# One change to a fused attention and expert-routing kernel: two routings search a grid with a proof, VectorE turns the rows, ScalarE reorders what is gathered

## The chip, the cores and the metric

The kernel runs on one core of a Trainium2 chip. That core has five engines that run their own instruction streams and wait for each other on semaphores: TensorE (PE in the profile, and PEld for its weight loads), VectorE (DVE), ScalarE (ACT), GpSimd (POOL) and SyncE (SP, which only issues DMAs here). The metric is the device time of one execution in microseconds (us), lower is better.

## The reference

Everything is float32. Attention with a sigmoid in the place of the softmax comes first; its output is regrouped to one row of 768 numbers for each of 3584 tokens; then a router gives each token to one of eight experts, each of which takes exactly 448 tokens.

```
q, k, v: 8 batches x 12 heads x 448 tokens x 64
attn = sigmoid(q k^T / 8 - log(448));  a = attn v
x = a regrouped to (8*448, 12*64) = (3584, 768)
logits = x @ w_gate                          # 3584 x 8
for idx in argsort(-logits.flatten()):       # best logits first
    tok, e = idx // 8, idx % 8
    if tok has an expert or expert e has 448 tokens: continue
    give tok to e
out[tokens of e] = relu(x[tokens of e] @ w1[e]) @ w2[e]   # 768 -> 1024 -> 768
```

The kernel does the greedy assignment one expert at a time: a token belongs to its best expert among those left, and the expert whose 448th best token has the highest logit is full first. It gets its tokens, is taken out, and the rest is routed again.

## The kernel before, in words

**Attention.** Batches and pairs of heads are walked in 48 iterations. VectorE turns the loaded q and k (`turn`, L408, tile `nkq` to `kqT`), ScalarE and VectorE split them in a high and a low part (L416, L417), TensorE makes the scores (`scores` L433, `rest_scores` L443), ScalarE the sigmoid (L423), TensorE the product with v (`av`, L457 and L463), VectorE copies it to SBUF (L465, L467) as `xt`: 128 head columns by 448 tokens. `logits` (L478) multiplies that with the gate. After each iteration one entry of a list `bg` is written, so small work is spread over the iterations.

**Rows.** The experts need rows by token, so `xt` is transposed and stored to the DRAM buffer `xs`. `rows` (L484) does half a chunk of 112 tokens: three TensorE transposes (L489), one copy (L492 by ScalarE or L494 by VectorE), and after the second half a DMA (L496). Batch 0 goes through `bg` during attention; the last `LATE = 7` batches, 56 half chunks, go to a list `late`, which is written between the steps of the first routing.

**Routing.** `Router.phase(k)` finds the k-th expert and its tokens. `keys` makes a key of each token for its best expert; `search` (L162) finds each expert's 448th largest key bit by bit: 16 steps, each with three thresholds counted by VectorE (L178), a sum over the partitions of an expert (for the first routing a TensorE matmul, L190; for the others VectorE transposes, L194 to L200), and a few one-column operations that set the next three thresholds. `pick` chooses the expert with the largest such key and the tokens at or above it, `place` and `lists` make the index list (`r_idx`, L298). SyncE reads the expert's number (`r_ei`) and loads its weights; GpSimd gathers the token rows from `xs` (L625).

**Experts.** For expert kx, `xturn` (L628) transposes the gathered rows by TensorE (L639) and splits them by ScalarE and VectorE; `moe` runs the two matrix products (L734 to L738 and L771 to L775), 144 matmuls each (the first of an expert in four groups of 36, the second in three of 48), and writes the result back through transposes and indirect DMAs. The generator `moe` yields after each matmul; a clock that adds 189 ns for each decides when a step of the next routing is written (`T_STEP`, `T_DVE` and the like are its due times), when gathers and transposes of the next expert are due (`prepare`, L820: gathers at once, transposes after a lag of 5 to 14 us, all left ones flushed at the end of the expert), so the program order is fixed when the kernel is built.

Of the kernel before, what the change touches and what calls it, by code (L numbers as in the profile page):

```python
# [36 lines left out]
Y_DVE, Y_WAIT = 6, 4000  # L37

# [10 lines left out]
def route_consts(nc, cp, K):  # L49
# [66 lines left out]
    K.gfin = _s32(g)  # L116


class Router:
# [4 lines left out]
    def __init__(self, tc, K, st, wk, psum):  # L124
# [5 lines left out]
        tc.nc.vector.memset(self.csum, -28.0)  # L130

# [30 lines left out]
    def search(self, pe):  # L162

        nc, K, wk, KT = self.nc, self.K, self.wk, self.KT
        p = self.bank()
        for g in range(2):
            nc.tensor.transpose(p[:, g * 112:(g + 1) * 112],
                                KT[:, g].rearrange("p e c -> p (e c)"), K.ident[:112, :112])
        KE = wk.tile([128, 224], F32, name="r_KE")
        nc.vector.tensor_copy(KE, p[:, :224])  # L170
        T, JP = K.c0, None
        X = None if pe else self.bank().bitcast(I32)
        for st in range(16):
            sh = 30 - 2 * st
            cnt = wk.tile([128, 3], BF, name="r_cnt") if pe else K.CN
            for i in range(3):
                junk = wk.tile([128, 224], BF, name="r_junk")
                nc.vector.tensor_scalar(junk, KE, T[:, i:i + 1].bitcast(F32), None, OP.is_ge, OP.add,  # L178
                                        accum_out=cnt[:, i:i + 1])
            nX = None  # L180
            if 0 < st < 15:
                nX = wk.tile([128, 3], I32, name="r_X") if pe else X[:, 4 * (st % 2):4 * (st % 2) + 3]
            acc = wk.tile([128, 1], F32, name="r_acc")
            j2 = wk.tile([128, 3], F32, name="r_j2")
            if pe:
                if nX is not None:
                    nc.vector.tensor_scalar(nX, K.kk[:, st + 1], JP, None, OP.bitwise_xor)
# [4 lines left out]
            else:  # L192
                ct = wk.tile([128, 32], F32, name="r_ct")
                nc.vector.transpose(ct, cnt)  # L194
                if nX is not None:
                    nc.vector.tensor_scalar(nX, K.kk[:, st + 1], JP, None, OP.bitwise_xor)
                s2 = wk.tile([128, 2], F32, name="r_s2")
                nc.vector.tensor_reduce(s2, ct.rearrange("p (e r) -> p e r", r=16), AX.X, OP.add)
                ct2 = wk.tile([128, 32], F32, name="r_ct")
                nc.vector.transpose(ct2.rearrange("p (e r) -> p e r", r=16), s2[:, :, None].to_broadcast([128, 2, 16]))  # L200
# [18 lines left out]
            if not pe:  # L219
                yield T_DVE  # L220
# [666 lines left out]
```

## Time and profile before

| what | value |
|---|---|
| median of 3 runs | 883.39 us (881.88 to 885.36) |
| profiled execution, whole time | 883.43 us |
| its span, first to last instruction | 881.7 us, granted clock 0.987 |
| PE busy | 840.1 us (95%) |
| DVE / ACT / POOL busy | 542.4 / 447.3 / 466.0 us |
| DMA traffic | 122.16 MB, mean 139 GB/s |
| attention (to the last `av`) | 0 to 278 us |
| first routing, gather and transposes | 278 to 333 us |
| eight experts | 333 to 862 us, then write-back |

"Busy" counts instructions in flight; a time in angle brackets after `<-` names what ended an idle time. All profile times are from the start of the span.

### The profile page before, as it was taken

How to read it: one execution, taken by the hardware profiler on the slowest of the kernel's cores; microseconds unless marked ns; L12 is line 12 of the kernel's file. 1: busy time of each engine (PE TensorE's matmuls, PEld its weight loads, DVE VectorE, ACT ScalarE, POOL GpSimd, SP SyncE). 2: the span in 40 equal slices, each digit the busy share in tenths (PEclk: the TensorE clock that was granted, in tenths of full speed). 3: DMA queues.
4: the chain of work that ended last, by engine and by line, in shares of the span. 5: the costliest groups of instructions: out<-in, count | busy, mean ns of one | idle time of the engine just before them, and what ended most of it. 6: DMA issues, size and time to landing. Idle time of an engine off the chain costs nothing.

```text
span 881.7 us, 16211 instructions
## 1 busy us (share of the span) xinstructions
PE 840.1 (95%) x5467; PEld 636.9 (72%) x5467; DVE 542.4 (62%) x2060; ACT 447.3 (51%) x612; POOL 466.0 (53%) x446
## 2 busy tenths in 40 slices
PE   6999999999999739998999999999999999999996
PEld 3455555555554528987988988988888888999996
DVE  4566555555554988958859879779779631332130
ACT  6777677777775734434434434534434344541420
POOL 9744344444410014854864873873883883851561
PEclk9999999999999979998999999999999999999999
DMA  9866766666621855443442442551542542634643
GB/s 173 165 142 149 153 126 127 127 126 127 126 43 54 270 192 154 120 138 123 128 136 97 160 155 81 177 162 57 189 153 72 170 153 90 209 96 141 203 151 126
DMA packets 213811, 122.16 MB, mean 139 GB/s; under 512 B 153344, under 2 KB 202496, under 8 KB 213728
## 3 DMA queue, kind: packets, MB, share of 16 engines
q1 hardware_dynamic: 200992, 87.62, 38.2%
q0 software_dynamic: 10880, 33.28, 12.0%
q8 instruction: 43, 0.70, 0.3%
q10 hardware_dynamic: 1856, 0.23, 0.2%
q14 instruction: 40, 0.33, 0.1%
HBM read 96.76 MB, written 24.31 MB: 137 GB/s over the span
## 4 chain that ended last, share of the span: by engine, by line
PE 82%; DVE 11%; issue 2%; DMA 2%; POOL 1%; SPq 1%; ACT 1%; POOLq 0%; DVEq 0%; ACTq 0%
PE tp L457 13%; PE sc L433 11%; PE sc L736 9%; PE sc L734 9%; PE sc L738 9%; PE sc L773 6%; PE sc L775 6%; PE sc L771 6%; DVE r_junk L178 4%; PE tp L463 2%; PE sc L443 2%; PE tp L639 2%; PE tp L652 2%; PE tp L478 1%; PE rt L289 1%
## 5 line engine op out<-in xcount | busy, mean ns | idle before, releaser
L605 POOL TENSOR_TENSOR wl<-wr,wh 128x768 fp32r<-128x768 f32 (+1 forms) x96 | 204.9, 2145 | 124.5 <-ACT wh L603 116.8
L423 ACT ACTIVATE at<-sc,bias 128x896 f32<-128x896 f32 x168 | 161.5, 1006 | 67.1 <-PE sc L443 38.4
L383 POOL DMA_DIRECT2D nkq<-in_q_dram x188 | 118.4, 646 | 116.2 <-DVE kqT L408 104.6
L775 PE MATMUL sc<-hh,wl 128*128 128x448 f32 (+2 forms) x400 | 150.2, 375 | 0.0
L738 PE MATMUL sc<-xh,wl 128*128 128x448 f32 (+2 forms) x396 | 146.2, 369 | 0.0
L736 PE MATMUL sc<-xl,wh 128*128 128x448 f32 (+2 forms) x396 | 146.0, 369 | 0.1
L773 PE MATMUL sc<-hl,wh 128*128 128x448 f32 (+2 forms) x400 | 145.5, 364 | 0.2 <-POOL hl L746 0.2
L734 PE MATMUL sc<-xh,wh 128*128 128x448 f32 (+2 forms) x396 | 145.0, 366 | 0.0
L771 PE MATMUL sc<-hh,wh 128*128 128x448 f32 (+2 forms) x400 | 144.1, 360 | 0.4 <-issue 0.4
L178 DVE TENSOR_SCALAR_CACHE_REDUCE r_junk<-r_KE,r_T 128x224 bf16<-128x224 f32 x315 | 123.2, 441 | 0.1
L603 ACT ACTIVATE wh<-wr 128x768 fp32r<-128x768 f32 (+1 forms) x112 | 102.0, 939 | 36.3 <-DMA wr<-in_moe_w_dram 23.4
L457 PE MATMUL tp<-at,nv 128*64 128x448 f32 x576 | 118.8, 548 | 0.0
L746 POOL TENSOR_TENSOR hl<-yt,hh 128x896 fp32r<-128x896 f32 x32 | 68.4, 2136 | 48.8 <-ACT yt L745 47.2
L742 ACT ACTIVATE hh<-sc 128x896 fp32r<-128x896 f32 x32 | 29.5, 921 | 117.1 <-PE sc L738 117.1
L417 DVE TENSOR_TENSOR kqL<-kqT,kqH 128x896 fp32r<-128x896 f32 (+1 forms) x49 | 52.5, 1073 | 58.5 <-ACT kqH L416 58.4
L773 PEld LDWEIGHTS sc<-hl,wh 128*128 128x128 f32 x400 | 75.8, 189 | 6.8 <-issue 1.1
L625 POOL DMA_INDIRECT xr<-xs,r_idx x32 | 32.0, 999 | 91.2 <-ACT wh L603 80.2
L736 PEld LDWEIGHTS sc<-xl,wh 128*128 128x128 f32 x396 | 75.2, 190 | 6.7 <-issue 0.5
L457 PEld LDWEIGHTS tp<-at,nv 128*64 128x64 f32 x576 | 37.1, 136 | 59.1 <-issue 56.6
L734 PEld LDWEIGHTS sc<-xh,wh 128*128 128x128 f32 x396 | 75.2, 190 | 6.0
L771 PEld LDWEIGHTS sc<-hh,wh 128*128 128x128 f32 x400 | 76.0, 190 | 4.8 <-issue 0.6
L738 PEld LDWEIGHTS sc<-xh,wl 128*128 128x128 f32 x396 | 75.1, 190 | 5.3
(166 smaller groups left out, 1266.1 us busy)
## 6 DMA issues: line engine op xcount, KB each, us to landing
wr<-in_moe_w_dram SPq DMA_DIRECT2D x64, 384.0 KB, 3.0
wr<-in_moe_w_dram SPq DMA_DIRECT2D x48, 512.0 KB, 3.6
nkq<-in_k_dram SPq DMA_DIRECT2D x192, 56.0 KB, 2.6
xs<-xr SPq DMA_DIRECT2D x32, 336.0 KB, 3.3
nkq<-in_q_dram POOLq DMA_DIRECT2D x188, 56.0 KB, 2.7
nv<-in_v_dram SPq DMA_DIRECT2D x92, 96.0 KB, 2.7
ys<-yt SPq DMA_DIRECT2D x20, 112.0 KB, 1.9
nr<-in_v_dram SPq DMA_DIRECT2D x46, 32.0 KB, 2.2
```

The costliest lines, as they stand in the source:

```text
L178: nc.vector.tensor_scalar(junk, KE, T[:, i:i + 1].bitcast(F32), None, OP.is_ge, OP.add, accum_out=cnt[:, i:i + 1])
L383: qn.dma_start(t[o:o + 32, n], rws[x])
L423: nc.scalar.activation(a, p[:, :, :S], AF.Sigmoid, bias=bias, scale=1 / math.sqrt(D))
L457: nc.tensor.matmul(p[j * 64:j * 64 + 64, :S], nat["v", b, g][:, h0 + j, c, :], AT[b, pr, c][:, j, :], start=(c == 0), stop=(c == 2 and pr ...
L603: nc.scalar.activation(hi, raw[u], AF.Copy)
L605: eng.tensor_tensor(lo, raw[u], hi.bitcast(F32), OP.subtract)
L734: nc.tensor.matmul(ph[:, f, lo:hi], wh[:, a, fs], xh[:, dd, lo:hi], start=st, stop=False)
L736: nc.tensor.matmul(ph[:, f, lo:hi], wh[:, a, fs], xl[:, dd, lo:hi], start=False, stop=False)
L738: nc.tensor.matmul(ph[:, f, lo:hi], wl[:, a, fs], xh[:, dd, lo:hi], start=False, stop=en)
L771: nc.tensor.matmul(py[:, d2, :w], wh[:, a, dsl], h1, start=st, stop=False)
L773: nc.tensor.matmul(py[:, d2, :w], wh[:, a, dsl], h2, start=False, stop=False)
L775: nc.tensor.matmul(py[:, d2, :w], wl[:, a, dsl], h1, start=False, stop=(j == 1 and a == 3))
```

## The change

Four things change together.

1. The first two routings use `grid_search`: thresholds on a fixed grid (4 steps for the first, from minus to plus twice a power of two `D` set by the largest logit of the first four batches; 9 steps for the second, in the distance `D` below the first routing's key). After it, `prove` counts the tokens at or above each expert's grid point: if exactly one expert has the highest point and exactly 448 tokens reach it, the point separates the same tokens as the exact key. VectorE reads that sum into a register and jumps over `exact`, the old search, which is run only otherwise. Routings 2 to 6 keep `search`.
2. Batches 0 to 6 are turned into rows by VectorE (`turn_rows`, three transposes of 32x32 blocks for each batch, written through `bg` during attention), batch 7 alone by TensorE in the gap (`late_rows`, with larger chunks). A row in `xs` now has its 768 numbers in the order (column of a block of 128, block) and not (block, column).
3. Since the order within a row is changed, expert 0 reads the gathered rows with a step of 6 in the transposes' weight load; for experts 1 to 7 ScalarE copies each gathered block into the plain order first (`order`, 28 copies, tile `xq`).
4. A 384-byte tile `pad` moves the load buffers: `nv`, `nr` and `nkq` start at byte 256 past a multiple of 512 in each partition before, and at a multiple of 512 now. Due times and buffer counts are set anew.

```diff
-LATE = 7
-XT_BUFS = 7
+LATE = 1
+XT_BUFS = 3
+XZ_BUFS = 2
-LATE_PER_STEP = 3
-LATE_KEYS = 7
+LATE_PER_STEP = 1
+LATE_KEYS = 3
+T_GRID, T_PROVE, T_FOUND = 2290, 3000, 9000
+N_FIRST, N_FAST = 4, 9
+PAD = 96
+NONE = 1.0e30
+FOUND = 0x43E00000
+FAST = 2
+ORDER = 2500
...
+    def grid_search(self, k):
+        nc, K, wk = self.nc, self.K, self.wk
+        pe = k == 0
+        rows = range(N_FIRST) if pe else range(1, N_FAST + 1)
+        if pe:
+            T, base = K.T0, K.base0
+        else:
+            base = wk.tile([128, 1], F32, name="r_base")
+            nc.vector.tensor_scalar(base, self.km, K.D, None, OP.subtract)
...
+        for r in rows:
...
+                self.count(T[:, i:i + 1], cnt[:, i:i + 1])
...
+            if pe:
+                ahead()
                 yield T_STEP
                 pc = self.bank()
                 nc.tensor.matmul(pc[:, :3], K.G, cnt, start=True, stop=True)
...
+            nc.vector.tensor_scalar(j2, tot, 447.5, None, OP.is_ge, OP.add, accum_out=acc)
+            if more:
+                T = wk.tile([128, 3], F32, name="r_T")
+                nc.vector.scalar_tensor_tensor(T, acc.to_broadcast([128, 3]), K.kw[:, r, :1], nX, OP.mult, OP.add)
+            nb = wk.tile([128, 1], F32, name="r_base")
+            nc.vector.tensor_scalar(nb, acc, K.kw[:, r, :1], base, OP.mult, OP.add)
...
+        self.count(base, self.cnt)
...
+    def prove(self, k):
+        p = self.bank()
+        nc.tensor.transpose(p[:, :128], self.base.to_broadcast([128, 128]), K.ident)
+        nc.tensor.matmul(p[:, 128:256], self.cnt.to_broadcast([128, 128]), K.G, start=True, stop=True)
...
+        nc.vector.tensor_scalar(few, cr, 447.5, NONE, OP.is_lt, OP.mult)
+        nc.vector.tensor_tensor(kr, tr, few, OP.subtract)
+        km = self.km = wk.tile([128, 1], F32, name="r_km")
+        nc.vector.tensor_reduce(km, kr, AX.X, OP.max)
+        nc.vector.tensor_tensor(few, cr, few, OP.add)
+        nc.vector.scalar_tensor_tensor(few, kr, km, few, OP.is_equal, OP.mult)
+        ok = wk.tile([128, 1], F32, name="r_ok")
+        nc.vector.tensor_reduce(ok, few, AX.X, OP.add)
+        found = nc.vector.value_load(ok[:1].bitcast(I32))
+        with self.tc.If(found != FOUND, preferred_fallthrough_block=True, label=f"found{k}"):
+            self.exact(kr)
+            nc.vector.tensor_reduce(km, kr, AX.X, OP.max)
+        self.choose(kr[:112], km[:112])
...
+        cp.tile([128, PAD], F32, name="pad")
...
+        def turn_rows(b, pr):
+            if pr == 1:
+                XR[b] = xa.tile([128, S // 32, 32, NP], F32, name="xz", bufs=XZ_BUFS)
+            nc.vector.transpose(XR[b].rearrange("p i j r -> p r i j")[:, pr - 1:pr + 1],
+                                XT[b][:, pr - 1:pr + 1].rearrange("p r (i t) -> p r i t", t=32))
+            if pr == NP - 1:
+                for a in range(4):
+                    nc.sync.dma_start(xs[b * S:(b + 1) * S, 192 * a:192 * a + 192].rearrange("(i t) c -> t i c", t=32),
+                                      XR[b][32 * a:32 * a + 32].rearrange("t i j r -> t i (j r)"))
...
+        def order(kx, j, n):
+            xq[kx, j] = xp.tile([128, DM], F32, name="xq", bufs=2)
+            nc.scalar.copy(xq[kx, j][:n].rearrange("p (r c) -> p r c", r=ND),
+                           xg[kx, j][:n].rearrange("p (c r) -> p r c", r=ND))
...
-                nc.tensor.transpose(p[:, i * n:(i + 1) * n], xg[kx, j][:n, dd * 128:(dd + 1) * 128], ident[:n, :n])
+                xc = xq[kx, j][:n, dd * 128:(dd + 1) * 128] if kx else xg[kx, j][:n, dd::ND]
+                nc.tensor.transpose(p[:, i * n:(i + 1) * n], xc, ident[:n, :n])
...
-                lag = max(5000, min(14000, start + 40000 - t0))
+                lag = max(ORDER + 5000, min(14000, start + 40000 - t0))
```

How the instruction order moves is seen at three places. The first is VectorE at the end of the first routing's search. `r_junk` is the count over `r_KE`, `rt` a PSUM bank, `r_J` the bits found so far, `r_km` the highest key. Before, steps 15 and 16 of 16 and the start of `pick`:

```order
L178 TENSOR_SCALAR r_junk,r_cnt<-r_KE,r_T 128x224 x3
L187 TENSOR_SCALAR r_X<-c_kk,r_J 128x3
L202 TENSOR_SCALAR r_j_3933,r_acc<-rt 128x3
L215 SCALAR_TENSOR_TENSOR r_T<-r_acc,r_X 128x3
L217 TENSOR_SCALAR r_J<-r_acc,r_J 128x1
L178 TENSOR_SCALAR r_junk,r_cnt<-r_KE,r_T 128x224 x3
L202 TENSOR_SCALAR r_j_3968,r_acc<-rt 128x3
L217 TENSOR_SCALAR r_J<-r_acc,r_J 128x1
L222 TENSOR_SCALAR r_kap<-r_J 128x1
L232 TENSOR_REDUCE r_km<-rt 112x1
L234 SCALAR_TENSOR_TENSOR r_w_3998<-rt,r_km,c_rank 112x8
```

Now, the fourth and last grid step, the proof and the jump (the 181 instructions of `exact` lie behind it, and the first of `choose` after those):

```order
L186 TENSOR_SCALAR r_junk,r_cnt<-r_KE,r_T 128x224 x3
L236 TENSOR_SCALAR r_j_3511,r_acc<-rt 128x3
L241 TENSOR_SCALAR r_base<-r_acc,c_kw,r_base 128x1
L186 TENSOR_SCALAR r_junk,r_cn_3518<-r_KE,r_base 128x224
L345 TENSOR_SCALAR r_few<-rt 128x8
L346 TENSOR_TENSOR r_kr<-rt,r_few 128x8
L348 TENSOR_REDUCE r_km<-r_kr 128x1
L349 TENSOR_TENSOR r_few<-rt,r_few 128x8
L350 SCALAR_TENSOR_TENSOR r_few<-r_kr,r_km,r_few 128x8
L352 TENSOR_REDUCE r_ok<-r_few 128x1
L353 TENSOR_LOAD r_ok
L354 COMPARE_AND_BRANCH
```

Twelve of sixteen steps are gone, and one count, six small operations, a register load and a jump have come.

The second is TensorE at the end of expert 0, where the gathered rows of expert 1 are transposed. Before (`xr` are gathered rows; L771 to L775 are expert 0, L734 to L738 expert 1):

```order
L639 MATMUL tp<-ident,xr 128x128 x3
L775 MATMUL sc<-hh,wl 128x448
L771 MATMUL sc<-hh,wh 128x448
L773 MATMUL sc<-hl,wh 128x448
L775 MATMUL sc<-hh,wl 128x448
L639 MATMUL tp<-ident,xr 128x128 x9
L639 MATMUL tp<-ident,xr 128x64 x6
L734 MATMUL sc<-xh,wh 128x448
```

Now (`xq` are the rows that ScalarE has reordered; L942 to L946 are expert 0, L905 to L909 expert 1), the last two of the eight groups of transposes:

```order
L810 MATMUL tp<-ident,xq 128x64 x3
L942 MATMUL sc<-hh,wh 128x448
L944 MATMUL sc<-hl,wh 128x448
L946 MATMUL sc<-hh,wl 128x448
L942 MATMUL sc<-hh,wh 128x448
L944 MATMUL sc<-hl,wh 128x448
L946 MATMUL sc<-hh,wl 128x448
L810 MATMUL tp<-ident,xq 128x64 x3
L942 MATMUL sc<-hh,wh 128x448
L944 MATMUL sc<-hl,wh 128x448
L946 MATMUL sc<-hh,wl 128x448
L905 MATMUL sc<-xh,wh 128x448
```

Before, five of the eight groups stood in one block between the experts; now all eight stand between matmuls of expert 0, because the second routing's list is written 42 matmuls earlier.

The third is VectorE in the middle of attention. Before, two iterations (L408 and L417 prepare the next pair, L465 and L467 take the result of the last):

```order
L408 STREAM_TRANSPOSE kqT<-nkq 128x896
L417 TENSOR_TENSOR kqL<-kqT,kqH 128x896
L465 COPY xt<-tp 128x448
L408 STREAM_TRANSPOSE kqT<-nkq 128x896
L417 TENSOR_TENSOR kqL<-kqT,kqH 128x896
L465 COPY xt<-tp 128x448
L467 TENSOR_TENSOR xt<-tp,xt 128x448
```

Now:

```order
L545 STREAM_TRANSPOSE kqT<-nkq 128x896
L554 TENSOR_TENSOR kqL<-kqT,kqH 128x896
L602 COPY xt<-tp 128x448
L655 STREAM_TRANSPOSE xz<-xt 128x2x448
L545 STREAM_TRANSPOSE kqT<-nkq 128x896
L554 TENSOR_TENSOR kqL<-kqT,kqH 128x896
L602 COPY xt<-tp 128x448
L604 TENSOR_TENSOR xt<-tp,xt 128x448
```

A row transpose stands ahead of every second `kqT`, 21 times in all. The stores of a batch's rows (four DMAs, L659) stand on SyncE's queue between the loads of later pairs.

More of the change, by code (lines that the diff above doesn't have):

```diff
@@ L167, in search @@
             nc.tensor.transpose(p[:, g * 112:(g + 1) * 112],
[L168 to L174, printed above, removed]
+                                KT[:, g].rearrange("p e c -> p (e c)"), self.K.ident[:112, :112])
+        self.KE = self.wk.tile([128, 224], F32, name="r_KE")
@@ new lines, in ends, with count, sums @@
+        nc.vector.tensor_copy(self.KE, p[:, :224])
+    def count(self, T, cnt):
+        junk = self.wk.tile([128, 224], BF, name="r_junk")
+        self.nc.vector.tensor_scalar(junk, self.KE, T, None, OP.is_ge, OP.add, accum_out=cnt)
+    def sums(self, cnt, ct, s2, ct2, between=None):
+        nc = self.nc
+        nc.vector.transpose(ct, cnt)
+        if between:
+            between()
+        nc.vector.tensor_reduce(s2, ct.rearrange("p (e r) -> p e r", r=16), AX.X, OP.add)
+        nc.vector.transpose(ct2.rearrange("p (e r) -> p e r", r=16), s2[:, :, None].to_broadcast([128, 2, 16]))
+        return ct2[:, :3]
@@ new lines, in grid_search, with search, ahead @@
+            nb = wk.tile([128, 1], F32, name="r_base")
+            nc.vector.tensor_scalar(nb, acc, K.kw[:, r, :1], base, OP.mult, OP.add)
+            base = nb
+            if more and not pe:
+                yield T_GRID
+        if pe:
+            self.tc.mark_branch_hint_location(f"found{k}", "LikelyTaken", [mybir.EngineType.DVE])
+        self.base = base
+        self.cnt = wk.tile([128, 1], BF, name="r_cn1")
+        self.count(base, self.cnt)
+    def search(self):
+        nc, K, wk = self.nc, self.K, self.wk
+        T, JP = K.c0, None
+        X = self.bank().bitcast(I32)
+        for st in range(16):
+            sh = 30 - 2 * st
+            for i in range(3):
+                self.count(T[:, i:i + 1].bitcast(F32), K.CN[:, i:i + 1])
+            nX = None
+            if 0 < st < 15:
+                nX = X[:, 4 * (st % 2):4 * (st % 2) + 3]
+            acc = wk.tile([128, 1], F32, name="r_acc")
+            j2 = wk.tile([128, 3], F32, name="r_j2")
+            def ahead(st=st, nX=nX, JP=JP):
@@ L329, in phase @@
             yield T_KEYS
-            yield from self.search(k == 0)
-            yield T_KAP
-            self.pick()
+            self.ends()
+            if k < FAST:
+                yield from self.grid_search(k)
+                yield T_PROVE
+                self.prove(k)
+                yield T_FOUND
+            else:
+                yield from self.search()
+                yield T_KAP
+                self.pick()
+                yield T_PICK
         else:
             self.left()
-        yield T_PICK
+            yield T_PICK
         yield from self.place()
@@ new lines, in moe_attention, with late_rows @@
+        XR = {}
+        def late_rows(b, c):
+            x = xa.tile([CP, DM], F32, name="xr", bufs=XA_BUFS)
+            p = ps_s.tile([128, 2, 512], F32, name="sc")
+            for r in range(NP):
+                o = r % 4 * 128
+                nc.tensor.transpose(p[:CP, r // 4, o:o + 128], XT[b][:, r, c * CP:(c + 1) * CP], ident)
+            xv = x.rearrange("p (c r) -> p r c", r=NP)
+            for h, n in ((0, 4), (1, 2)):
+                nc.scalar.copy(xv[:, 4 * h:4 * h + n], p[:CP, h, :128 * n].rearrange("p (r c) -> p r c", r=n))
+            nc.sync.dma_start(xs[b * S + c * CP:b * S + (c + 1) * CP], x)
@@ L531, in moe_attention @@
                     bg.append(lambda b=b: logits(b, range(NP)))
-                for c in range(NCH):
-                    for hf in range(2):
-                        if b >= B - LATE:
-                            late.append(lambda b=b, c=c, hf=hf: rows(b, c, hf, "act"))
-                        else:
-                            bg.append(lambda b=b, c=c, hf=hf: rows(b, c, hf, "dve"))
+                if b == 3:
+                    bg.append(scale)
+                for c in range(NCH if b >= B - LATE else 0):
+                    late.append(lambda b=b, c=c: late_rows(b, c))
         for f in bg:
```

141 lines of the change are left out of this document (97 added, 44 removed).

## The prediction

> **What bounds the kernel now.** I read the table of stages first (from, to, length, then busy time and instruction count of PE, PEld, DVE, ACT and POOL, granted clock, DMA share, GB/s).
>
> ```profile
> 0.00:278.00 278.00, 270.40 (x2216) 137.88 (x2216) 152.35 (x210) 199.82 (x220) 128.30 (x220) 1.00 0.62 126
> 278.00:333.00 55.00, 34.47 (x257) 23.05 (x257) 45.48 (x223) 29.85 (x63) 4.13 (x6) 0.88 0.68 218
> 333.00:400.00 67.00, 66.86 (x399) 59.86 (x398) 53.60 (x284) 26.23 (x39) 41.09 (x22) 1.00 0.45 137
> 400.00:412.00 12.00, 9.36 (x39) 7.40 (x39) 9.42 (x50) 4.59 (x10) 2.97 (x4) 0.72 0.13 45
> 412.00:862.00 450.00, 446.93 (x2462) 397.30 (x2461) 279.77 (x1296) 184.63 (x277) 285.43 (x187) 1.00 0.44 140
> ```
>
> Attention and the experts are TensorE's: it idles 7.6 us of 278 and 3.1 of 450. The two stages in which it is not the bound are the gap of 55 us, where DVE is busy for 45, and the 12 us around 400, with the clock at 0.72. The chain of waits (start, length, what) says what fills the gap:
>
> ```profile
> 285.12 0.52 DVE r_junk L178 x3
> ...
> 287.66 1.20 DVE r_junk L178 x6
> ...
> 311.75 1.11 DVE r_junk L178 x6
> ...
> 313.60 1.11 DVE r_junk L178 x6
> ...
> 326.70 4.49 DMA xr<-xs,r_idx
> ```
>
> The sixteen search steps follow one another at 1.85 us (313.60 - 311.75) with nothing between, then the token list, then the gather. The row transposes of seven batches that PE does meanwhile (L489) are only cover: nothing in the chain after 285 is theirs.
>
> **First routing.** The timeline (start, length, engine, line; in brackets the idle time and its releaser) ends the search so:
>
> ```profile
> 315.97 0.17 DVE L232 TENSOR_REDUCE r_km<-rt 112x1 f32<-112x8 f32 x1 [0.41 <-PE rt L229]
> 316.17 0.23 DVE L234 SCALAR_TENSOR_TENSOR r_w<-rt,r_km,c_rank 112x8 f32<-112x8 f32 x1
> 316.43 0.16 DVE L236 TENSOR_REDUCE r_c<-r_w 112x1 f32<-112x8 f32 x1
> 316.62 0.23 DVE L239 TENSOR_SCALAR rt<-r_w,r_c 112x8 f32<-112x8 f32 x1
> 318.29 0.13 DVE L249 TENSOR_SCALAR r_ei<-r_c 1x1 int32<-1x1 f32 x1
> 319.79 20.22 SPq L592 DMA_DIRECT2D wr<-in_moe_w_dram  x8
> ```
>
> From the first count to `r_w`, which both kernels have next, is 316.17 - 285.12 = 31.05 us. Now: four steps, 7.4; one more count, 0.5 (its row below: 441 + 85 ns); the PE turn between two DVE instructions, 0.4 (the 0.41 in brackets); six small operations at the 0.24 us that L232 to L239 are apart, 1.4; the register load, 0.8. The load is an estimate from SyncE's reading of `r_ei`: written at 318.42, it lets the first weight DMA go at 319.79, and of these 1.4 us I give a good half to the load and the rest to address and issue. That is 10.5 us before the jump.
>
> ```profile
> L178 DVE TENSOR_SCALAR_CACHE_REDUCE r_junk<-r_KE,r_T x45: 435/441/446, 287.7 to 314.2; 128x224 bf16<-128x224 f32 x45
> L178 DVE DVE_READ_ACCUMULATOR r_junk<-r_KE,r_T x45: 83/85/88, 288.0 to 314.6; 128x1 bf16 x45
> xs<-xr SPq DMA_DIRECT2D x32, 336.0 KB, 3.3
> ys<-yt SPq DMA_DIRECT2D x20, 112.0 KB, 1.9
> q8 instruction: 43, 0.70, 0.3%
> ```
>
> No row has a jump over code. Its cost lies between nothing (the code is there) and a wait for code from memory: a DMA lands in 1.9 to 3.3 us, and one code packet (0.3% of 16 engines times 881.7 us, over 43) keeps an engine for about 1.0, so 4.3 at most. I take 2.0, the shortest landing, since the jump passes 181 instructions: 12.5 us in all, 18.5 saved (16.2 to 20.5).
>
> [...]
>
> `late_rows` now puts six transposes, not three, ahead of those that start the router, and six cost about 0.5 us more than three (rows of the next part): 18.0 saved. The four late chunks end early in the gap, and no weight load, gather or store of the old chain is passed by: SyncE issues its last store now four chunks in, not at 315. Behind the jump everything keeps its order, with weights and gather that much earlier. PE stands idle longer, but its clock fell in the gap already (0.88 on average, second row), so it starts the experts no colder than before.
>
> **Attention.** Batch 0's rows leave PE, on its path:
>
> ```profile
> 50.00:104.00 54.00, 4.31 (x24) 2.36 (x24) 1.00 0.71 150
> 56.40 0.53 PE tp L489 x3
> 61.39 0.47 PE tp L489 x3
> ```
>
> Eight such pieces at 0.50 are 4.0 us; one transpose for the grid's scale comes back, 0.3: 3.7 saved. In their place DVE gets 21 transposes of 128x896, a few us of constants aside. Their price:
>
> ```profile
> L408 DVE STREAM_TRANSPOSE kqT<-nkq 128x896 f32<-128x896 f32 x47 | 51.8, 1103 | 2.5 <-DMA nv<-in_v_dram 1.5 <-DMA nkq<-in_k_dram 0.2
> L669 DVE STREAM_TRANSPOSE yt<-sc 128x896 f32<-128x896 f32 x5 | 5.6, 1118 | 32.5 <-PE sc L775 25.0 <-issue 7.5
> 230.06 0.62 DVE L465 COPY xt<-tp 128x448 f32<-128x448 f32 x1 [0.53 <-PE tp L457]
> 230.60 1.10 DVE L408 STREAM_TRANSPOSE kqT<-nkq 128x896 f32<-128x896 f32 x1
> 231.80 0.95 ACT L416 ACTIVATE kqH<-kqT 128x896 fp32r<-128x896 f32 x1
> 232.66 1.89 ACT L423 ACTIVATE at<-sc,bias 128x896 f32<-128x896 f32 x2
> 232.78 1.09 DVE L417 TENSOR_TENSOR kqL<-kqT,kqH 128x896 fp32r<-128x896 f32 x1 [1.08 <-ACT kqH L416]
> 236.10 2.09 PE sc L433 x18
> ```
>
> L669 writes with a step of two elements and costs no more than L408, so I take 1.1 us at a step of six, 23 in all beside DVE's 152 of 278. The place counts more: each stands between L465 and the next `kqT`. Queued behind it are `kqT`, then ScalarE's L416 and its two sigmoids, then `kqL`, all 1.1 us later: `kqL` ends at 235.0, and the scores that need it start at 236.10. About 2.1 us are covered, so this costs 0 at 1.1 and, from 2.1 on, 21 times the rest. The stores of six more batches (8.3 MB) move from the gap into attention; at the gap's rate (218 GB/s at a share of 0.68, 320 at full) they are 26 us of all engines and lift the share from 0.62 to about 0.72. Behind them on SyncE's queue wait loads that the code issues four iterations ahead (48 take 278 us, 5.8 each), so some us of delay stay hidden. The alignment could shorten loads; only the first are waited for, and I give it 0 (up to 0.5 gained).
>
> **Second routing.** Of the seven steps fewer nothing is on PE's path, but the list is written 42 matmuls earlier, so no block of transposes is left between expert 0 and expert 1:
>
> ```profile
> 401.88 1.01 PE L639 MATMUL tp<-ident,xr 128*128 128x128 f32 x6 [1.08 <-DVE xl L643]
> 403.60 0.87 PE L639 MATMUL tp<-ident,xr 128*128 128x128 f32 x6 [0.71 <-DVE xl L643]
> 405.32 0.58 PE L639 MATMUL tp<-ident,xr 64*128 64x64 f32 x3 [0.85 <-DVE xl L643]
> 406.57 0.37 PE sc L736
> 411.44 0.21 PE sc L736
> ```
>
> There PE idles 2.64 us, and then its clock is down and some 12 matmuls take 0.37 in the place of 0.21, 2.0 more: 4.6 saved (2 if the gather or the reordering comes late there, 6 if later lists, which are earlier too, also mend part of the 3.1). If VectorE is late with this proof, PE waits at the proof's matmuls or at `place`; the latter stands 42 matmuls, 8.6 us, behind the jump's place.
>
> **Reordering and jumps.** ScalarE gets 28 copies of 128x768, nearest row:
>
> ```profile
> L603 ACT ACTIVATE wh<-wr 128x768 fp32r<-128x768 f32 x64 | 52.8, 847 | 26.6 <-DMA wr<-in_moe_w_dram 23.4 <-PE sc L773 3.2
> ```
>
> 28 x 0.85 = 24 us beside 184.63 busy of 450. Each waits for its gather, and behind it on ScalarE wait the splits of weights, the relu and the evacuations that free PE's banks. The order leaves twelve matmuls (2.5 us) between a copy and the transposes that read it, enough for it and one 1.0 us split. I take 1.5 us on PE's path, between 0 and 8 (a third of the 24). The stepped weight loads of expert 0's 24 transposes and the jumps of the four other engines over no code: 0.5, between 0 and 3.
>
> **Sum**, against the profiled execution's 883.4 (span 881.7), which is the median of the runs: 883.4 - 18.0 - 3.7 - 4.6 + 1.5 + 0.5 = 859.
>
> **Rivals.**
> *ScalarE becomes what TensorE waits for.* Against it: 59% idle. For it: its queue is in order, and waits for weights alone (23.4 us in the row) hold all that stands behind. At half of the copies' time, 12 us in the place of 1.5: 869.
> *Jumps cost the most that the rows allow*, 4.3 on VectorE and 3 on the others: 859 + 2.3 + 2.5 = 864. [...]
> *VectorE stalls attention (slower).* If the step of six makes a transpose several times as dear, each one over 2.1 us holds `kqL` and with it the scores. At 4.4 us, four times L408: 21 x 2.3 = 48, so 907; it decides for slower from 3.3 us (24.4 gained, over 21, above 2.1). Against it: L669's step costs 15 ns.
> *The proof fails*, and the old search runs behind the grid: 16 steps at 1.85 or more, plus 17 small operations at 0.24, 34 us, so 893. Against it: worked out from the reference's inputs, the batches' tokens lie in tight clusters; the first expert's 448th logit is 0.01120, its grid point 0.01099, and exactly 448 tokens lie above; the second's is 0.00997646 with the 449th at 0.00997589, ten times the last grid step apart.
>
> **Chances and range.** Forecast (852 to 866) 0.68, with the jump rival inside it at 0.10; ScalarE 0.14; better than 852, 0.06; stalled attention 0.06; failed proof 0.03; else 0.03. The likeliest one's own range is 852 to 866. For 8 in 10 I give 851 to 871, which takes in most of the ScalarE case and leaves the two slow ones out. A measurement of this kernel can tell about 0.5% (4 us) from no change: faster 0.89, within 0.5% 0.02, slower 0.09.
>
> **What would show it.** Right: four counts of three in the gap, the gather's list about 18 us after the first count, not 39; no L489-like transposes between 50 and 104; no idle PE or lower clock at the end of expert 0; `xz` transposes near 1.1 us. Wrong: a DVE hole over 2 us behind the register load; PE idle before scores in attention; PE waiting for `xq` or for banks in the experts; a second search behind the grid.

## The result, and the profile after

The changed kernel takes 878.12 us (median of 9 runs, 873.60 to 880.83) against 883.63 (9 runs, 881.88 to 885.62) for the one before: a ratio of 0.9936, 95% interval 0.9915 to 0.9958. It is 0.6% faster, some 5.5 us, where the forecast had 24.4. The profiled execution is the fastest of the nine: 873.60, span 871.8. So the trace shows a gain of 9.9 us of span, while the median gained 5.5; the 4.5 us between this execution and the median have to be explained beside it.

The table of stages of the changed kernel (columns as in the prediction):

```profile
0.00:278.00 278.00, 268.08 (x2193) 135.01 (x2193) 183.76 (x240) 201.35 (x220) 128.16 (x220) 1.00 0.74 155
278.00:313.00 35.00, 11.12 (x102) 8.28 (x102) 26.10 (x96) 9.43 (x15) 4.20 (x6) 0.61 0.34 105
313.00:380.00 67.00, 66.15 (x395) 59.12 (x394) 50.42 (x240) 32.68 (x43) 41.06 (x22) 1.00 0.44 132
380.00:392.00 12.00, 12.00 (x67) 10.34 (x66) 11.31 (x72) 5.31 (x12) 4.89 (x6) 1.00 0.27 85
392.00:852.00 460.00, 446.40 (x2439) 395.25 (x2438) 275.41 (x1226) 219.19 (x299) 284.30 (x186) 0.99 0.43 136
```

Attention is as long as before. The gap is 35 us and not 55. The 12 us between expert 0 and expert 1, which had 9.36 us of PE at a clock of 0.72, are now full. But the last row, which was 450 us with 3.1 us of TensorE idle, is 460 with 13.6 idle: half of what the gap gave is lost in the experts. The two jumps in the timeline of the changed kernel (`r_ok` is the last operation ahead of the first one, `r_w` the first behind each):

```profile
294.52 0.16 DVE L352 TENSOR_REDUCE r_ok<-r_few 128x1 f32<-128x8 f32 x1
296.06 0.23 DVE L362 SCALAR_TENSOR_TENSOR r_w<-r_kr,r_km,c_rank 112x8 f32<-112x8 f32 x1 [1.38 <-DVEq L354]
350.13 0.23 DVE L362 SCALAR_TENSOR_TENSOR r_w<-r_kr,r_km,c_rank 112x8 f32<-112x8 f32 x1 [4.83 <-DVEq L354]
```

and the turned and the reordered rows in its groups (busy, mean ns, idle before):

```profile
L655 DVE STREAM_TRANSPOSE xz<-xt 128x896 f32<-128x896 f32 x21 | 38.9, 1852 | 0.0
L795 ACT COPY xq<-xr 128x768 f32<-128x768 f32 (+1 forms) x28 | 46.4, 1657 | 2.8 <-issue 1.6 <-DMA xr<-xs,r_idx 1.2
```

A turn costs 1.85 us, not 1.1; a reordering copy 1.66, not 0.85; register load and jump 1.38 in the first routing and 4.83 in the second. TensorE's waits in the expert stage (total, times, longest), in the changed kernel:

```profile
PE tp L810 <- DVE xl L814: 7.5, 6, 3.4
PE rt L417 <- DVE r_oh L412: 3.8, 2, 2.7
PE tp L810 <- ACT xq L795: 1.6, 4, 0.6
```

and before:

```profile
PE tp L639 <- DVE xl L643: 4.2, 5, 1.1
PE rt L289 <- DVE r_oh L284: 0.3, 1, 0.3
```

In these rows TensorE's transposes (`tp`) wait for VectorE to empty their bank (`xl`) or for ScalarE's reordered rows (`xq`), and the list matmuls (`rt`) wait for `r_oh`. The waits that grew most name VectorE, not ScalarE. What VectorE, GpSimd and TensorE do in the timeline of the changed kernel around one such hole:

```profile
673.86 2.13 POOL L917 TENSOR_TENSOR hl<-yt,hh 128x896 fp32r<-128x896 f32 x1
675.94 3.60 POOL L769 TENSOR_TENSOR wl<-wr,wh 128x768 fp32r<-128x768 f32 x2
...
675.59 5.04 DVE L412 TENSOR_TENSOR r_oh<-c_io,r_rr 112x2048 f16<-112x2048 int16 x1
...
677.63 0.37 PE L905 MATMUL sc<-xh,wh 128*128 128x448 f32 x1
680.69 1.12 PE L417 MATMUL rt<-r_oh,c_mv 112*32 112x64 f16 x32 [2.69 <-DVE r_oh L412]
681.74 0.74 PE L907 MATMUL sc<-xl,wh 128*128 128x448 f32 x1
```

`r_oh` is a comparison that takes 1.215 us alone. Here it begins while GpSimd is subtracting and ends at 680.63, 1.09 us after the last of three subtractions (675.94 + 3.60 = 679.54). TensorE, whose list matmuls wait for it, stands 2.69 us, and the matmul behind them takes 0.74 us, for 0.37 ahead of the hole. So I had two theories: **R**, ScalarE's copies at twice their price hold its queue; **V**, VectorE's routing operations are shut out by GpSimd, and the change has moved them to where TensorE waits.

### The profile page after: what moved, and what is told of

Its sections match the earlier page's. It is cut to its first block, busy times and chain, and to the rows that moved or that the text cites. A ratio compares the mean times of both kernels' runs of the same rounds, so it can differ in the third digit from the quotient of the medians.

```text
span 871.8 us, 15601 instructions
## 1 busy us (share of the span) xinstructions
PE 816.0 (94%) x5290; PEld 619.6 (71%) x5290; DVE 548.9 (63%) x1872; ACT 470.1 (54%) x592; POOL 466.7 (54%) x446
## 4 chain that ended last, share of the span: by engine, by line
PE 42%; DVE 11%; issue 2%; ACT 2%; POOL 1%; DMA 1%; POOLq 0%; ACTq 0%; DVEq 0%
PE sc L907 7%; PE sc L905 7%; PE sc L909 7%; PE sc L946 6%; PE sc L944 6%; PE sc L942 6%; DVE r_junk L186 3%; PE tp L823 2%; PE tp L810 1%; DVE r_oh L412 1%; PE rt L417 1%; DVE r_Ti L280 1%; DMA xr<-xs,r_idx 1%; ACT xq L795 1%; POOL out_dram L861 1%
## 5 line engine op out<-in xcount | busy, mean ns | idle before, releaser
L946 PE MATMUL sc<-hh,wl 128*128 128x448 f32 (+2 forms) x400 | 150.0, 375 | 0.0
L909 PE MATMUL sc<-xh,wl 128*128 128x448 f32 (+2 forms) x396 | 145.6, 368 | 0.0
L942 PE MATMUL sc<-hh,wh 128*128 128x448 f32 (+2 forms) x400 | 144.8, 362 | 0.4 <-ACT yt L874 0.4
L905 PE MATMUL sc<-xh,wh 128*128 128x448 f32 (+2 forms) x396 | 145.0, 366 | 0.0
L186 DVE TENSOR_SCALAR_CACHE_REDUCE r_junk<-r_KE,r_Ti 128x224 bf16<-128x224 f32 x225 | 88.0, 441 | 0.2
L942 PEld LDWEIGHTS sc<-hh,wh 128*128 128x128 f32 x400 | 76.3, 191 | 4.6 <-ACT yt L874 0.6
L946 PEld LDWEIGHTS sc<-hh,wl 128*128 128x128 f32 x400 | 76.2, 191 | 4.3
L905 PEld LDWEIGHTS sc<-xh,wh 128*128 128x128 f32 x396 | 74.9, 189 | 5.6
L909 PEld LDWEIGHTS sc<-xh,wl 128*128 128x128 f32 x396 | 74.9, 189 | 5.2
```

Source lines behind the costliest of these rows:

```text
L186: self.nc.vector.tensor_scalar(junk, self.KE, T, None, OP.is_ge, OP.add, accum_out=cnt)
L905: nc.tensor.matmul(ph[:, f, lo:hi], wh[:, a, fs], xh[:, dd, lo:hi], start=st, stop=False)
L909: nc.tensor.matmul(ph[:, f, lo:hi], wl[:, a, fs], xh[:, dd, lo:hi], start=False, stop=en)
L942: nc.tensor.matmul(py[:, d2, :w], wh[:, a, dsl], h1, start=st, stop=False)
L946: nc.tensor.matmul(py[:, d2, :w], wl[:, a, dsl], h1, start=False, stop=(j == 1 and a == 3))
```

## The experiments

Ratios are to the kernel before in the same series, since its median differs a little (882 to 883.6) from series to series.

| run | median us (range) | ratio, 95% interval |
|---|---|---|
| the change | 878.12 (873.60 to 880.83) | 0.9936, 0.9915 to 0.9958 |
| stepped | 879.03 (874.0 to 879.94) | 0.9941, 0.9921 to 0.9961 |
| psum_operand | 865.43 (862.59 to 867.37) | 0.9811, 0.9798 to 0.9824 |
| before_psum | 881.13 (879.6 to 883.44) | 0.9982, 0.9970 to 0.9994 |
| second_by_search | 873.06 (872.0 to 875.15) | 0.9897, 0.9883 to 0.9912 |
| psum_second_by_search | 870.85 (870.13 to 873.08) | 0.9870, 0.9852 to 0.9888 |
| turn_unstepped | 872.13 (870.54 to 876.52) | 0.9883, 0.9864 to 0.9902 |
| psum_lines16 | 864.38 (863.5 to 866.28) | 0.9796, 0.9778 to 0.9813 |
| psum_stepped | 867.34 (863.59 to 867.81) | 0.9818, 0.9797 to 0.9840 |
| psum_short_jump | 870.37 (867.61 to 872.05) | 0.9868, 0.9849 to 0.9887 |
| psum_short_aligned | 862.20 (861.74 to 863.14) | 0.9778, 0.9763 to 0.9793 |
| psum_pad256 | 865.29 (862.62 to 867.84) | 0.9810, 0.9788 to 0.9831 |
| proof_psum | 874.67 (873.16 to 876.59) | 0.9907, 0.9886 to 0.9928 |
| psum_proof | 862.99 (862.65 to 863.32) | 0.9773, 0.9753 to 0.9792 |
| psum_proof_stepped | 863.15 (862.81 to 864.01) | 0.9777, 0.9757 to 0.9797 |
| all_mended | 861.00 (860.25 to 861.54) | 0.9759, 0.9744 to 0.9773 |

### ScalarE's copies, or VectorE shut out by GpSimd

`stepped` takes the copies away:

```diff
-                xc = xq[kx, j][:n, dd * 128:(dd + 1) * 128] if kx else xg[kx, j][:n, dd::ND]
+                xc = xg[kx, j][:n, dd::ND]
...
-                        if i + 1 < len(bl):
-                            order(kx + 1, *bl[i + 1])
```

> No ScalarE reordering at all: experts 1 to 7 read the gathered rows with a step of six in the transposes' weight load, as expert 0 does. In the profile of the change the 28 copies took 1668 ns each (47 us of ScalarE), and the expert stage was 10 us longer than forecast or more. Theory R (the copies hold ScalarE's queue, and that is where the gain went): the expert stage gives back most of it, 868 to 872. Theory V (VectorE's list and search operations are stretched to 3.4 to 5.0 us when a GpSimd subtraction runs, and that is where it went): no gain, and the stepped loads (227 ns against 189 to 199 in expert 0) add 168 x 0.03 = 5 at most: 876 to 883.

`psum_operand` leaves the copies and gives two VectorE operations one operand in PSUM (`P` is a bank of it, `nX` there a copy of `kk[:, 1]`; `r_rr` is float32 in the bank and int16 before, so with the place the type changes too):

```diff
-        rr = wk.tile([112, 32], I16, name="r_rr")
+        rr = P[:, 320:352] if k else wk.tile([112, 32], I16, name="r_rr")
...
-                nc.vector.tensor_scalar(T, K.kk[:, 1], nJ, None, OP.bitwise_xor)
+                nc.vector.tensor_scalar(T, nX, nJ, None, OP.bitwise_xor)
```

> Two VectorE operations of each later routing read one operand from PSUM and not both from SBUF: the comparison that writes r_oh (1215 ns alone, 3429 and 5044 beside GpSimd), which loses its 16-bit speed (estimate 2.2 us by 2048 elements at one each 1.04 ns, from 1215 for two), and the first threshold r_Ti (228 ns alone, up to 4230); one small copy to PSUM is added to each search. Theory V: none of them is over 2.5 us, TensorE's waits for r_oh (2.69 the longest) and its idle of 2 to 3 us around 565 and 675 go, 870 to 873. Theory R: 876 to 880, TensorE's idle times in the experts stay.

Without the copies, and with stepped loads in their place: 879.03, nothing gained; the longest `r_oh` and `r_Ti` of its trace are still 4.99 and 4.24 us. With the operands in PSUM: 865.43, 0.0125 in the ratio or 11 us, better than even V had it. The instructions on these two tiles (count: shortest, median, longest ns), in the changed kernel:

```profile
L412 DVE TENSOR_TENSOR r_oh<-c_io,r_rr x8: 1215/1216/5044, 301.2 to 691.1; 112x2048 f16<-112x2048 int16 x8
L280 DVE TENSOR_SCALAR r_Ti<-c_kk,r_J x5: 228/853/4230, 369.3 to 624.8; 128x3 int32<-128x3 int32 x5
```

and in `psum_operand`:

```profile
L412 DVE TENSOR_TENSOR r_oh<-c_io,rt x7: 2275/2277/2278, 355.8 to 680.2; 112x2048 f16<-112x2048 int16 x7
L280 DVE TENSOR_SCALAR r_Ti<-rt,r_J x5: 220/221/221, 369.2 to 618.5; 128x3 int32<-128x3 int32 x5
```

The comparison is now 1.06 us dearer each time and never longer than 2.28, the first threshold never longer than 0.22, and together that is worth 11 us. The table of busy times over the expert stage, first matmul to last, says where they were; changed kernel, then `psum_operand`:

```profile
313.00:864.00 551.00, 536.14 (x2995) 476.11 (x2994) 338.62 (x1537) 258.67 (x357) 332.37 (x217) 0.99 0.43 136
```

```profile
313.00:853.00 540.00, 532.90 (x2995) 473.53 (x2994) 333.85 (x1542) 259.29 (x357) 329.32 (x217) 1.00 0.43 138
```

TensorE's idle time falls from 14.9 to 7.1 us, and its busy time for the same matmuls by 3.2, which fits the slow matmuls behind each hole (0.74 for 0.37 above). Both traces have their first expert matmul at 312.85; the last starts at 863.90 in the change and at 852.78 here. Followed matmul by matmul, 4.4 of these 11.1 us arise from 568 to 576 of the change's time, behind the `r_Ti` that takes 4.23 us from 557.91 on, and 4.1 from 677 to 686, behind the `r_oh` of 5.04. `before_psum` makes the same edit in the kernel before.

> The kernel before with the same two VectorE operations reading one operand from PSUM. Its trace too has stretched ones (r_oh 3019 and 2643 in the place of 1212), but TensorE idles only 3.1 us from 412 to 862. Theory V (the same stalls are harmless where the schedule leaves room, and the change moved them to places where TensorE waits): 881 to 883. Rival (they cost before as much as in the change, so psum_operand's 12.7 us are no part of the change's result): 872 to 877.

It measured 881.13, ratio 0.9982: 1.6 us. The kernel before had the same collisions (its longest `r_oh` was 3019 ns), at places where TensorE waited for little. The change did not bring them in; it moved the routing's operations, so that some met longer stretches of GpSimd's subtractions (5.04 for 3.02 us) at places where the list is needed at once. With both inputs in SBUF `r_oh` took 1215 to 5044 ns and `r_Ti`, int32 in either place, 228 to 4230; with one input in PSUM all seven `r_oh` took 2275 to 2278, in `psum_operand` as in `before_psum`, and all five `r_Ti` 220 to 221. How GpSimd's subtractions hold the others up no run shows. And `r_oh` at 675.59 lost not to one GpSimd instruction but to three in a row.

### What the second grid search is worth

`second_by_search` sets `FAST = 1`, so the second routing uses the old search; `psum_second_by_search` does it with the operands in PSUM.

```diff
-FAST = 2
+FAST = 1
```

> The second routing goes by the old search of 16 steps; all else as changed. The forecast put 4.6 us on this part (TensorE's idle block and slow clock between expert 0 and expert 1). If that holds the time is 882 to 883 (878.1 + 4.6), with the idle block back at about 380 to 392. Rival: the earlier second list has only moved all later lists to worse places beside GpSimd's subtractions, what was gained at the boundary is lost behind it, and the time is 875 to 879.

> psum_operand with the second routing by the old search. If the forecast's term for the boundary between expert 0 and 1 (4.6 us) holds once no VectorE operation is stretched, the time is 869 to 871 with TensorE idle in a block of transposes around 380 to 390. Rival: the boundary's transposes only move elsewhere, 864.5 to 867.

In the change, the second grid search makes the kernel slower: without it 873.06, 5 us less. This was better than either theory had it. With the stretched operations mended, it makes it faster: 865.43 with it, 870.85 without, 5.4 us. That this lies near the 4.6 of the forecast is partly chance: 865.43 still holds the race that a later section shows, which the kernel without a second jump does not have. With the race gone too (`psum_proof`, 862.99), the difference is about 8 us.

The same four runs say what moved the operations. The two operands in PSUM are worth 11 us with the second grid search and 2.4 without it (0.9897 to 0.9870), and 1.6 in the kernel before. In the trace of `second_by_search` the longest `r_oh` is 3009 ns and the longest `r_Ti` 1235, as before the change (3019 and 1240), not 5044 and 4230. Without it, the timeline of `second_by_search` has the idle block between the experts back:

```profile
381.79 0.52 PE L810 MATMUL tp<-ident,xq 128*128 128x128 f32 x3 [1.18 <-ACT xq L795]
383.50 0.55 PE L810 MATMUL tp<-ident,xq 128*128 128x128 f32 x3 [1.19 <-DVE xl L814]
384.74 0.55 PE L810 MATMUL tp<-ident,xq 128*128 128x128 f32 x3 [0.69 <-ACT xq L795]
```

The forecast's mechanism was right; its price was that the later lists, written earlier, met GpSimd elsewhere.

### The step of six

`turn_unstepped` writes the turned blocks side by side.

```diff
-            nc.vector.transpose(XR[b].rearrange("p i j r -> p r i j")[:, pr - 1:pr + 1],
+            nc.vector.transpose(XR[b][:, pr - 1:pr + 1],
```

> The 21 VectorE transposes write without the step of six (the numbers within a row then stand in another order, so the rows that the experts read are left wrong; the bytes stored and the DMAs' shapes are the same). In the profile of the change one takes 1852 ns, the unstepped ones of q and k 1103. If the step makes the price, it falls to 1.1 us, VectorE is busy 16 us less in attention, and the waits of scores for the sigmoid (29.9 us over 58 in the weight loads' row, 13.9 before) fall back. Theory: these waits ate attention's 3.7 us, so the last addition comes 2 to 4 us earlier, 874 to 876. Rival: the DMA share of 0.74 or the routing's grid scale (1.8 us at 160 to 180) ate them, and attention ends at 277 to 278 as now.

`psum_lines16` keeps the rows usable: groups of four columns stay together (ScalarE now reorders expert 0's blocks as well).

```diff
-            nc.vector.transpose(XR[b].rearrange("p i j r -> p r i j")[:, pr - 1:pr + 1],
-                                XT[b][:, pr - 1:pr + 1].rearrange("p r (i t) -> p r i t", t=32))
+            nc.vector.transpose(XR[b].rearrange("p i c r j -> p r (i c) j")[:, pr - 1:pr + 1],
+                                XT[b][:, pr - 1:pr + 1].rearrange("p r (c j) -> p r c j", j=4))
```

> On top of psum_operand, a row in xs has its 768 numbers in the order (group of four columns, block, column in the group): VectorE's turn, the late rows and ScalarE's reordering then step over runs of four floats, 16 bytes, and not over single ones. [...] If that is the cause, the turn falls from 1852 to about 1103 ns and the copy from 1668 to about 847; attention ends 2.3 us earlier (as with turn_unstepped), the first expert waits some 1 us for its copies, and with 865.4 for psum_operand it is 862 to 865. Rival: any write in pieces costs the same, the durations stay near 1.85 and 1.67, and the time is 865 to 868.

The groups of `psum_lines16`:

```profile
L795 ACT COPY xq<-xr 128x768 f32<-128x768 f32 (+1 forms) x32 | 26.6, 830 | 8.6 <-DMA xr<-xs,r_idx 8.6
L655 DVE STREAM_TRANSPOSE xz<-xt 128x896 f32<-128x896 f32 x21 | 23.1, 1102 | 0.0
```

The whole time is 864.38, within its theory. For the turn, runs of four floats cost as much as no step at all (1102 ns, and 1101 in `turn_unstepped`); single floats at a step of six cost 1.7 times that in the turn (1852), and in ScalarE's copy twice the 830 of runs of four (1657). Why single floats cost more no run shows. In the row on which the prediction rested, L669 took 1118 ns at a step of two floats; that did not carry over to a step of six. What the dearer turn did to attention shows at its last addition (timeline), in the changed kernel:

```profile
277.93 0.62 DVE L604 TENSOR_TENSOR xt<-tp,xt 128x448 f32<-128x448 f32 x1 [3.03 <-PE tp L600]
```

and in `turn_unstepped`:

```profile
275.58 0.62 DVE L604 TENSOR_TENSOR xt<-tp,xt 128x448 f32<-128x448 f32 x1 [3.03 <-PE tp L600]
```

The step is 2.35 of the 3.7 us that attention should have gained. The median of `turn_unstepped` fell by more, to 872.13, below its theory's 874. Its profiled execution, 872.39, is only 1.2 us faster than the change's; how much of the rest is the race of a later section no run shows. Another 1.25 of the 3.7 is in the wait for the grid's scale, for which I had counted the transpose (0.29) and not what it waits for; no run takes this wait away. Timeline of the changed kernel:

```profile
162.68 0.29 PE L626 MATMUL tp<-ident,s_m 128*128 128x128 f32 x1 [1.25 <-DVE s_m L624]
174.52 0.48 PE L570 MATMUL sc<-kqL,kqH 64*128 64x448 f32 x2 [0.53 <-DVE kqL L554]
```

The second row is a turn that holds `kqL`, as the prediction described it, but for 0.53 us only; with the cheaper turn of `psum_lines16` this hole is gone. A wait of 0.5 for `xt` (L602) is gone in `turn_unstepped` too; by which waits the rest of the 2.35 us came about is open.

### The jump, and where the load buffers lie

`psum_short_jump` drops the call `self.exact(kr)`, the body that VectorE jumps over (it is not executed with these inputs).

> psum_operand without the body that VectorE jumps over (the old search as the way out; the jump itself and the reduction behind it stay). The register load and jump took 1.38 us in the first and 4.8 us in the second routing. If the wait is for code behind the 181 instructions, the second falls to 1.4 or less; if it is the register load or the queue, it stays at 4.8. The time: within 1 us of 865.4 either way, unless the executions' spread (0.5 to 0.8%) comes from that wait, then the runs lie closer together.

The second jump fell from 4.76 to 0.78 us, the first from 1.38 to 1.0, so most of the second wait comes with the body that is jumped over. What is waited for there no run shows, nor why the first jump over the same 181 instructions cost so much less, 1.38 us. But the time rose, to 870.37, where I had expected it within 1 us of 865.4: attention ended 5.4 us later. The dropped body's tiles had shifted the load buffers to 64 bytes past a multiple of 512. Two runs set their place: `psum_short_aligned` back to a multiple of 512 (`PAD = 208`), and `psum_pad256` gives `psum_operand` the 256 past that the kernel before had (`PAD = 32`).

> psum_short_jump with the load buffers back at a multiple of 512 bytes (pad 448 bytes larger). If the place of the buffers made attention 5.2 us longer there, it ends at 278.5 again, the second jump is at 0.8 us, and the time is 863 to 866. Rival (something else in that program): attention stays at 283 to 284 and the time at 869 to 871.

> psum_operand with the load buffers at 256 past a multiple of 512 bytes, as before the change (the tile pad is 128 bytes, not 384). The forecast gave alignment 0: 864 to 867 as psum_operand (865.4), attention ends at 278.5. Rival: in psum_short_jump the buffers lay at 64 past a multiple of 512, because the tiles of the body left out were gone, and attention ended at 283.8 with a DMA share of 1.11 in the place of 0.81 from 20 to 60; if any distance from a multiple of 512 costs, attention ends 1 to 5 us later, 867 to 870.

The busy table from 20 to 60 (DMA share and GB/s at the end), `psum_short_jump`:

```profile
20.00:60.00 40.00, 37.66 (x272) 18.06 (x270) 26.10 (x36) 28.23 (x32) 24.69 (x49) 1.00 1.11 148
```

`psum_short_aligned`:

```profile
20.00:60.00 40.00, 39.47 (x324) 19.57 (x322) 27.95 (x45) 29.49 (x33) 25.04 (x51) 1.00 0.82 172
```

At 64 the same loads keep the DMA engines busy for more of the time (1.11 for 0.82) and move fewer bytes (148 for 172 GB/s), and attention starves; at 0 and at 256 there is no difference (865.43 and 865.29, both with a share of 0.81 and 172 GB/s from 20 to 60). So the alignment in the change is worth 0, as forecast. Why 64 costs and 256 does not no run shows.

With the place corrected the short jump gives 862.20, 3.2 us under `psum_operand`, and the runs lie within 1.4 us, not 4.8. But the fastest runs of `psum_operand` and `psum_pad256` (862.59 and 862.62) are as fast with the long jump. So the second jump had to do with the spread, more than with the shortest time.

### A race of 0.4 us behind the second jump

The first operation behind that jump, `r_w`, has two SBUF inputs, and GpSimd begins a subtraction just there. Timeline of `psum_operand`'s profiled execution:

```profile
350.05 0.23 DVE L362 SCALAR_TENSOR_TENSOR r_w<-r_kr,r_km,c_rank 112x8 f32<-112x8 f32 x1 [4.76 <-DVEq L354]
...
350.18 4.74 POOL L769 TENSOR_TENSOR wl<-wr,wh 128x1024 fp32r<-128x1024 f32 x2
```

and of `psum_stepped`'s:

```profile
350.80 2.10 DVE L362 SCALAR_TENSOR_TENSOR r_w<-r_kr,r_km,c_rank 112x8 f32<-112x8 f32 x1 [5.22 <-DVEq L354]
...
350.48 4.71 POOL L769 TENSOR_TENSOR wl<-wr,wh 128x1024 fp32r<-128x1024 f32 x2
...
354.95 0.19 PE L385 MATMUL rt<-c_ones,r_mk 112*64 112x1 bf16 x1 [2.31 <-DVE r_ei L377]
```

0.13 us ahead of GpSimd it costs nothing; 0.32 behind, it ends at 352.90, about where the first of the two subtractions does (half of 4.71 behind 350.48), and TensorE stands for 2.31 us. The whole price is higher. `psum_pad256` was profiled at 867.28 with `r_w` 2.26 long, `psum_operand` at 862.59 with 0.23. Followed matmul by matmul, the expert stage of `psum_pad256` lags by 0.9 us ahead of the hole and by 4.6 a few microseconds after it, so the race costs 3.8: the hole, and slow matmuls after it (the granted clock from 345 to 360 is 0.89 for 1.00). The change's profiled execution (`r_w` at 350.13, 0.23 long) was of the first kind, that of `stepped` (879.93, `r_w` 2.29) of the second. `proof_psum` is the change with the row `r_kr` in PSUM:

```diff
-        few, kr = wk.tile([128, 8], F32, name="r_few"), wk.tile([128, 8], F32, name="r_kr")
+        few, kr = wk.tile([128, 8], F32, name="r_few"), p[:, 256:264]
```

> The change with one edit: the proof's key row r_kr lies in PSUM, so the two VectorE operations around the second jump have one operand in SBUF (load buffers kept at a multiple of 512 bytes). In two traces the operation behind that jump started 0.13 us before a GpSimd subtraction (0.23 us long, no hole) or 0.32 us behind its start (2.10 us, and TensorE stood 2.31 us). Theory: the change's profiled execution (873.6, its fastest) was of the first kind and most others of the second, so this edit alone brings the median to 873 to 875, with executions within 2 us or so of each other, and leaves the later stalls (r_oh 3.4 and 5.0, r_Ti 4.2). Rival: the spread has another source, 876 to 879 and as wide as the change's (7 us).

It measured 874.67, a median within the theory; the ratio moves by 0.0029 (2.6 us), but its interval overlaps the change's, and the runs still spread over 3.4 us (7.2 in the change), more than the 2 that the theory had. At 3.8 us the race would fill most of the 4.5 between the change's fastest run and its median. How many of the change's runs lost it is not shown, nor what else varies there, only that with the later stalls mended too (`psum_proof`) the spread is 0.7. All edits together, with `psum_lines16`:

> psum_lines16 with the proof's key row r_kr in PSUM too, so that the two operations around the second jump (2.03 and 2.45 us there, 0.23 alone) have one operand in SBUF; load buffers at a multiple of 512. Theory V: neither is stretched, TensorE's 2.3 us hole at 352 goes, 861 to 863 against 864.4 for psum_lines16. Rival: the hole comes from the jump's 4.8 us alone, 863.5 to 865.5.

861.00: ratio 0.9759, faster than the change and than the kernel before by more than any interval. Two runs then settle the copies on this quiet ground:

> psum_operand without ScalarE's reordering (all experts read by stepped weight loads). Theory R, second part (beside the VectorE stalls, now gone, the copies still hold ScalarE's queue): 861 to 863.5 against 865.4. Rival (the copies are covered; each stepped load adds some tens of ns): 865 to 870, with TensorE's transposes longer.

> psum_operand and proof_psum together, rows as in the change (step of six, copies of 1.67 us). all_mended was 861.0 with the cheaper turn and copies. Theory: the cheaper turn is worth its 1.8 to 2.4 us of attention less about 1.4 that the first expert waited for ScalarE there, so 861 to 863. Rival: the copies of 1.67 us cost more than that, 863 to 866.

> psum_proof without ScalarE's reordering. On this quieter ground the price of the 28 copies is the difference to psum_proof. The forecast gave the copies 1.5 on TensorE's path against 24 stepped loads at 0.5 or less for all edits together; theory: within 1 us of psum_proof, either way. Rival: the copies do hold up ScalarE's queue, 2 us or more below psum_proof.

`psum_stepped` against `psum_operand` was undecided (867.34 and 865.43, both spread over 4 us by the race). `psum_proof` and `psum_proof_stepped` differ by 0.2 us: the 28 copies and the stepped loads cost TensorE the same. They are not free, though. TensorE waits 4.5 us ahead of the transposes of the gathered rows (L810) in `psum_proof`, and 1.5 in `psum_proof_stepped`, so the copies cost about 3, and the longer weight loads as much. Between `psum_proof` and `all_mended` the medians differ by 2.0 and the runs do not overlap, though the ratios' intervals do; in ratios it is 1.2. So the cheaper turn and copies are worth 1 to 2 us together; attention ends 2.3 us earlier.

## Why the prediction was wrong

In ratios, with 883.4 as the unit: the forecast was 0.9724, the change 0.9936, 18.7 us apart. Of these `proof_psum` takes back 2.6 (0.9936 to 0.9907), the two operands on top of it 11.8 (to 0.9773), the cheaper turn and copies 1.2 (to 0.9759), and 3.1 are left, which no run divides; each ratio is uncertain by about 1.8 us.

The step that failed is in the sum itself: but for the copies' 1.5 it let the experts take as long as before or less, since it gave nothing to VectorE operations that come to stand elsewhere beside GpSimd. In place of that nothing the runs showed `r_oh` and `r_Ti` stretched to 5.04 and 4.23 us, which TensorE waits for, and 11 us that come back when they read one operand from PSUM.

- **First routing, -18.0: right, a little too small.** From the first count (284.88) to `r_w` (296.06) it is 11.2 us; the forecast had 12.5, before the change it was 31.05. Attention ends at the same time in both, and TensorE's first expert matmul starts at 312.85 in the place of 332.80: 19.95 us saved. The term that was off is the first jump with its register load, 1.38 for the 2.8 assumed; why it was so cheap, when the jump over as many instructions in the second routing took 4.83, is open, so this part was luck.
- **Attention, -3.7: wrong, 0.** "L669 writes with a step of two elements and costs no more than L408, so I take 1.1 us at a step of six" failed: 1.85. And "about 2.1 us are covered" was wrong too, since 1.85 should then have been free, and going back to 1.1 gained 2.35 us. The wait for the grid's scale, 1.25, had no term. 2.35 and 1.25 are the 3.7, nearly; the first is shown by a run, the second read from the trace.
- **Second routing, -4.6: the mechanism right, the sum wrong.** The block between expert 0 and 1 went, and on mended ground the step is worth 5.4 us, or about 8 without the race, more than the 4.6. In the change it costs 3 to 5 (0.9936 with it, 0.9897 without). The failing step is "of the seven steps fewer nothing is on PE's path": all later lists move as well, and an earlier VectorE operation is not always an earlier result. The forecast had a bound for later lists that improve, and none for ones that get worse.
- **Reordering, +1.5: too small; stepped loads, +0.5: in expert 0 not measured alone.** The copies took twice the assumed duration (1.66) and cost TensorE about 3 us of waits, not 1.5: at L810 it waits 9.1 us in the change and 6.0 in `stepped`. Taking them away gained nothing, with or without the stalls, because stepped loads in their place cost as much.
- **Alignment, 0: right** for 256 against 512.
- **The rivals.** ScalarE was not what TensorE mostly waits for, though its 869 (869.6 by its own terms) lay nearer to the result than 859 did: a rival can come closer in time by another's mechanism. The second jump, 4.83, is over the 4.3 that I took as the most the rows allow. With the race behind it, it costs about 3 us (865.43 to 862.20); by itself less, since `psum_proof`, which mends the race and keeps a jump of 3.4, lies 0.8 above `psum_short_aligned`. VectorE did stall attention, by a twentieth of that rival's price. The proof held in both routings. What decided was no rival at all, though the trace of before showed it (shortest, median, longest):

```profile
L284 DVE TENSOR_TENSOR r_oh<-c_io,r_rr x8: 1212/1436/3019, 321.3 to 712.8; 112x2048 f16<-112x2048 int16 x8
```

I did not ask why the longest is 2.5 times the shortest, and what would happen if it stood elsewhere.

## What to carry to other kernels

Before an operation is moved in time, look at the longest, not only the mean duration of every group on its engine: a VectorE operation with 1.2 us at best and 3.0 at worst may be shut out by another engine, as here by GpSimd, and a new schedule decides who waits for it. One operand in PSUM took that risk away for 1.06 us a list and was worth 11 us. And a layout with a step was priced here by how much stays together: four floats kept side by side took the copy from 1.66 to 0.83 us and the turn from 1.85 to 1.10.

## What the runs showed of the hardware that I had not expected

- A VectorE operation of 128x3 integers (0.228 us) took 4.23 beside two GpSimd subtractions, and `r_oh` 5.04 beside three: each ended only behind the last of them, by 0.04 and 1.09 us.
- The outcome of such a meeting turns on tenths of a microsecond: 0.13 us ahead, 0.23 us; 0.32 behind, 2.10, and with it some 3.8 us of the expert stage.
- A jump over 181 instructions took 1.38 us in one place and 4.8 to 5.2 in the other; with the body gone, 1.0 and 0.8. With `r_kr` in PSUM it was 3.4 to 3.6, which I cannot explain.
- Load buffers at 64 bytes past a multiple of 512 made attention 5.4 us longer, at a DMA share of 1.11 for 0.82; 256 past made no difference.
